# Linear attention and a gated MLP on one core: half units in pairs, twelve gated units, and TensorE for part of the first two batches

## The chip, the cores and the metric

The kernel runs on one core of one Trainium2 chip. The metric is the device time in microseconds of one execution. A core has five engines that the text names: TensorE (PE in the profile, with its weight loads as PEld), VectorE (DVE), ScalarE (ACT), GpSimd (POOL) and SyncE (SP, which issues nearly all DMAs here).

## What is computed

```python
q_s = softmax(q, axis=-1)            # over the 64 features of a row
k_s = softmax(k, axis=2)             # over the 576 rows of the sequence
kv  = einsum('bhsd,bhse->bhde', k_s, v)
x   = einsum('bhsd,bhde->bhse', q_s, kv)   # then (batch, row) x (8 heads * 64)
h   = x @ w_in
g   = h * sigmoid(beta * h)
out = g @ w_out
```

There are 8 batches, 8 heads, 576 rows and 64 features a head, so x has 4608 rows of 512; w_in is 512 x 2048 and w_out 2048 x 512. All inputs and the output are float32. The kernel writes g as (tanh(beta' h) + 1) h with the halves put into the constants.

## The kernel before, in words

**The work.** The sequence of a batch is split as row = 9 p + i, with p on 64 partitions and i from 0 to 8; two heads share the 128 partitions, so a batch has four blocks j of two heads. Of each batch, the rows i = 0 to 7 make one chunk of 512 tokens for the MLP, and the rows i = 8 of all batches together make one more (chunk 7, the tails; batch 7's own rows are chunk 8). A chunk has 16 units, one for each 128 columns of w_in: unit n multiplies xT by w_in into a PSUM bank (`st1`, line 758, operation `h_n`), ScalarE takes the tanh (`tanh`, line 774, `th_n`), VectorE forms the gated unit (`gate`, line 787, `g_n`) and TensorE multiplies it by w_out into the four output banks acc (`st2`, line 825, `o_n`). There are 9 x 16 = 144 units, each of four `h` matmuls and four `o` matmuls of 512 columns.

**The attention of batch b** goes through these operations: `ld_q`, `ld_k`, `ld_v` (line 259, each half a batch, 576 KB); `qmax` (360), `qsub` (376, GpSimd), `qexp` (383), `qsum` (406), `qrcp` (412, 413), `qnorm` (421, GpSimd) and then q transposed, `qT_b` (line 428): for batches 1 to 7 by one DMA that SyncE issues, for batch 0 by TensorE (`qtr`, line 442) with copies out of PSUM (`qtrev`); `qtrt_0` and `qtrtev_0` do its row i = 8. For k: `kmax` (462), `kred`, `ksmall`, `krep` (515, which lays the maximum, kmb, over the partitions), `ksub` (525), `kexp` (532). For batch 0 three of the four blocks' `ksub` are VectorE's and one GpSimd's, and `kswap_0` (479) is a small float32 product on TensorE. `vcast` makes v bfloat16. `kv_b` (556) gives k_s' v, `kvn_b` (575 to 578, VectorE) divides it, `x_b` (606) multiplies it with the transposed q, four `xev` copy the result to xT, and `xt_b` (645), `xtev` do the same for row i = 8.

**The order** is written out by hand in `ORDER`, a list of some 1200 names; each engine runs its own operations in that order and waits by semaphores. SyncE's order of loads, transposes and stores is part of it, as is the engine that a copy runs on (`=act`, `=dve`, `=pool`). Names with `fill` are matmuls on zeros or on exponentials that keep TensorE at work in the first 21 us; nothing reads them.

**Buffers.** PSUM has four banks `acc` for the outputs and a ring of four (`take`) for everything else: a `h` unit, a `kv` (two), an `x` half (two), an `xt` (two), a transposed q. A bank is free when the operation that empties it is done. `g` has NG = 8 buffers, so a gate waits for the `o` of the unit eight before; `th` has three. The output of a chunk is copied from acc to osb (`oev`) and stored (`st`, line 854) in two DMAs for each 128 tokens, one for each of the two rows i that the block holds.

**The first four units** (LEAD) work on halves of 256 tokens, since xT of batch 0 comes in halves: `h_n_half_x` are two of the four products, `th_n_half` and `g_n_half` take 256 columns each, and a unit holds one bank for both of its halves. The last eight units split their `o` by output block, and the last block (`oev_8_3`, `st_8_3`) by halves.

**The maximum of q in the first block** (SUMMED): for one of batch 0's parts ScalarE takes the maximum as a bias and sums as it goes (`q_exp_sum`, eight small activations for each block).

Of the kernel before, what the change touches and what calls it, by code (L numbers as in the profile page):

```python
# [22 lines left out]
krep_0_0, krep_0_1, ksub_0_2=dve, ksub_0_0=dve, qnorm_0_0_1=pool, vcast_0_j0=act, qexp_0_2_1, qsum_0_2_1,
vcast_0_j1=act, ksub_0_3=pool, vcast_0_j2=pool, fill_15, ld_q1_1, qrcp_0_1, fill_4, fill_14, qtrev_0_0_0=act,
kexp_0_2, qtr_0_0_1, kexp_0_3, kexp_0_0, ld_w0_1, ld_w0_0, ld_k1_1, ksub_0_1=dve, kexp_0_1, fill_16, kv_0_1, beta_ev,
kv_0_0, qmax_1_3, cast_w0_0_1=act, qmax_1_2, ld_w1_0, ld_w2_0, qnorm_0_1_0=pool, qnorm_0_1_1=pool, qtr_0_1_0,
qtr_0_1_1, fill_3, kvn_0, cast_w0_1_1=act, qtrev_0_1_0=act, qtrev_0_0_1=dve, x_0_0_1, x_0_0_0, xev_0_0_0=act,
cast_w0_1_0=pool, fill_5, qrcp_0_2, qtrev_0_1_1=dve, cast_w0_0_0=pool, xev_0_0_1=dve, qsub_1_1=pool, fill_7, x_0_1_1,
x_0_1_0, h_0_0_0, h_0_0_1, h_2_0_0, xev_0_1_0=act, qnorm_0_2_1=pool, kmax_1_3, xev_0_1_1=dve, th_0_0, g_0_0, h_3_0_0,
fill_6, cast_w2_0=pool, h_3_0_1, qexp_1_3, qnorm_0_2_0=pool, th_3_0, ld_w2_1, qexp_1_2, h_1_0_0, h_1_0_1, h_0_1_0,  # L30
h_2_0_1, cast_w1_0=pool, cast_w2_1=pool, ld_w1_1, h_2_1_0, h_2_1_1, h_0_1_1, h_3_1_0, th_1_0, h_1_1_0, ld_k1_0,
h_1_1_1, h_3_1_1, ld_w4_1, qsum_1_3, ld_w4_0, kmax_1_2, th_0_1, qsum_1_2, g_0_1, ld_w3_0, th_2_0, th_1_1, th_2_1,
ld_q1_0, ld_w3_1, o_0_0, th_3_1, g_3_0, g_2_0, g_2_1, qrcp_1_1, o_0_1, h_5, cast_w1_1=pool, qnorm_1_1=pool, ld_w6_1,
cast_w4_1=pool, g_3_1, g_1_0, g_1_1, kmax_1_1, kmax_1_0, kred_1, th_5, ksmall_1, h_4, g_5, o_1_0, th_4, h_6, th_6,
krep_1, g_4, o_1_1, h_7, o_2_0, o_2_1, o_3_0, cast_w4_0=pool, g_6, cast_w3_0=act, h_8, th_7, th_8, ld_w5_0, qmax_1_0,
qmax_1_1, ld_w6_0, ksub_1_0=pool, o_3_1, h_9, th_9, qsub_1_0=pool, h_11, o_4, cast_w3_1=act, o_5, o_6, g_7, o_7, g_8,
ld_w5_1, ld_q2_1, h_10, cast_w5_0=pool, cast_w6_1=act, th_11, ld_v1_1, qexp_1_1, ld_w7_0, o_8, g_11, qexp_1_0, g_9,
qsum_1_0, qsum_1_1, ksub_1_1=pool, cast_w6_0=act, th_10, qtrt_0, qtrtev_0_0=act, h_12, cast_w5_1=act, kexp_1_3, o_9,
h_14, kexp_1_0, th_12, qtrtev_0_1=dve, qrcp_1_0, kexp_1_1, th_14, g_10, qmax_2_2, qmax_2_3, qnorm_1_0=pool, h_15,
h_13, ld_v1_0, ld_w7_1, cast_w7_0=act, g_14, g_12, th_13, g_13, vcast_1_1=pool, qsub_2_1=pool, kexp_1_2, th_15, g_15,  # L40
vcast_1_0=pool, o_10, o_11, qexp_2_3, qexp_2_2, o_12, o_13, cast_w7_1=pool, qsum_2_3, kv_1_0, kv_1_1, o_14, qT_1,
kvn_1, qsum_2_2, x_1_1, x_1_0, xev_1_2=act, xev_1_0=dve, xev_1_3=dve, xev_1_1=act, qrcp_2_1, ld_q2_0, o_15, h_17_0,
qmax_2_0, ld_v2_1, ld_k2_1, ld_k2_0, h_17_1, qmax_2_1, oev_0_3=act, th_17, ld_q3_0, h_16_0, g_17, h_16_1, th_16,
g_16, ld_v2_0, ld_k3_0, h_18, th_18, oev_0_2=act, g_18, kmax_2_3, h_24, oev_0_0=act, h_21, th_21, kmax_2_0,
qnorm_2_1=pool, kmax_2_1, h_20, oev_0_1=act, qsub_2_0=pool, g_21, h_19, o_16, o_17, h_22, th_20, kmax_2_2, o_18,
qmax_3_0, g_20, th_19, g_19, ld_v3_0, qexp_2_1, th_24, th_22, kred_2, ksmall_2, vcast_2_1=pool, h_23, g_22, krep_2,
ld_k3_1, th_23, qmax_3_1, g_23, qexp_2_0, kmax_3_2, ld_q3_1, h_26, st_0_1, o_19, o_20, h_25, vcast_2_0=act, g_24,
qsum_2_1, kmax_3_3, ld_q4_0, o_21, h_27, qsum_2_0, th_26, o_22, vcast_3_0=pool, ksub_2_1=pool, kexp_2_2, th_25, g_26,
g_25, kexp_2_3, ksub_2_0=pool, th_27, o_23, g_27, ld_v3_1, o_24, o_25, xt_0, kexp_2_0, kexp_2_1, kv_2_0, kv_2_1,
xtev_0_0=act, xtev_0_1=act, h_30, h_28, kmax_3_0, qrcp_2_0, qnorm_2_0=pool, kmax_3_1, qsub_3_0=pool, qmax_3_2, kvn_2,  # L50
qmax_3_3, kred_3, th_30, th_28, g_28, st_0_3, qsub_3_1=pool, vcast_3_1=pool, h_29, o_26, ld_q4_1, h_31, st_0_0,
ld_k4_1, st_0_2, th_29, ksmall_3, g_29, g_30, qT_2, th_31, o_27, o_28, o_29, g_31, krep_3, x_2_1, xev_2_3=act, x_2_0,
xev_2_0=dve, xev_2_2=dve, qexp_3_1, ld_k4_0, o_30, o_31, xev_2_1=act, kmax_4_1, qexp_3_2, h_34, oev_1_2=act, th_34,
ksub_3_0=pool, ksub_3_1=pool, h_32, oev_1_1=dve, th_32, oev_1_3=act, qmax_4_1, h_33, oev_1_0=act, th_33, qexp_3_3,
g_34, g_32, ld_v4_1, h_35, qsum_3_1, ld_v4_0, th_35, st_1_1, ld_q5_1, h_37, h_36, qmax_4_3, kexp_3_3, g_33, th_36,
qmax_4_2, th_37, g_35, qmax_4_0, o_32, g_37, qsum_3_2, g_36, vcast_4_1=pool, vcast_4_0=pool, h_38, kexp_3_0, o_33,
th_38, h_39, qsum_3_3, qsub_4_1=pool, qexp_3_0, kexp_3_1, qsub_4_0=pool, th_39, g_39, qrcp_3_1, h_42, o_34, qsum_3_0,
# [58 lines left out]
def kernel(  # L116
# [629 lines left out]
    def st1(n, ks=(0, 1, 2, 3), h=None):  # L746
# [8 lines left out]
        if ("h", n) not in place:  # L755
            take(("h", n))
# [169 lines left out]
```

## Time and profile before

| | us |
|---|---|
| median of 3 runs | 293.31 (292.52 to 293.66) |
| the profiled execution's own time | 294.5 |
| its span, from the first to the last instruction | 292.7 |
| first `h` matmul on TensorE | 20.96 |
| last matmul ends | 288.04 |
| TensorE busy | 276.3 |
| VectorE, ScalarE, GpSimd busy | 199.6, 170.4, 130.7 |

Busy times are of the engine over the whole span. In a row of the order of time stand the start, the time, the engine, the line, the operation, what it writes and reads with the shape, the count, and in brackets the idle time of the engine just before it and what ended that. SPq, ACTq mean that the engine's sequencer issues a DMA. In a row of groups stand, after the bar, the busy time of all and the mean ns of one, then the idle time before them. PEclk is the granted share of TensorE's clock.

### The profile page before, as it was taken

Reading aid. Unit: us, or ns where it says so; the run is one execution under the profiler, and the core shown is the slowest. Engines: PE = TensorE matmul, PEld = TensorE weight load, DVE = VectorE, ACT = ScalarE, POOL = GpSimd, SP = SyncE. Lnnn points to the kernel's source line nnn. Section 1 sums busy time; section 2 is a strip of 40 time slices with the busy share of each in tenths; the row PEclk is TensorE's granted clock in tenths of the full one; section 3 lists DMA queues with packets and bytes.
Section 4 is the critical chain, followed back from the end, with each engine's and each line's share of the span. In section 5 each row is a group of like instructions: output and inputs, shape, how many; then the busy total and the mean of one; then the engine's idle time right before and its main releaser. Section 6 shows DMA issues by size and latency. Waiting matters only on the chain.

```text
span 292.7 us, 5174 instructions
## 1 busy us (share of the span) xinstructions
PE 276.3 (94%) x1922; PEld 128.7 (44%) x1951; DVE 199.6 (68%) x414; ACT 170.4 (58%) x297; POOL 130.7 (45%) x92
## 2 busy tenths in 40 slices
PE   7589999999999999996999999999999999999993
PEld 2255444444444544443344444444444444445551
DVE  3898867899799989774598968654754362456250
ACT  3687797866596656681375456845754255245342
POOL 5698986737987292661816473742002000000000
PEclk9889999999999999999799999999999999999999
DMA  7999999999954860699466908200410450005006
GB/s 247 392 391 385 386 380 208 394 383 357 231 185 155 209 215 0 176 229 304 164 204 226 179 23 164 61 2 0 111 34 2 81 125 21 0 1 129 17 0 143
DMA packets 39736, 50.60 MB, mean 173 GB/s; under 512 B 18576, under 2 KB 18848, under 8 KB 39712
## 3 DMA queue, kind: packets, MB, share of 16 engines
q1 hardware_dynamic: 39552, 50.15, 57.3%
q8 instruction: 15, 0.25, 0.3%
q10 hardware_dynamic: 160, 0.13, 0.2%
q14 instruction: 9, 0.07, 0.1%
HBM read 36.71 MB, written 9.44 MB: 158 GB/s over the span
## 4 chain that ended last, share of the span: by engine, by line
PE 73%; DMA 9%; DVE 6%; ACT 4%; issue 2%; SPq 2%; POOL 1%; POOLq 1%; ACTq 0%; DVEq 0%
PE hT L758 36%; PE acc L825 33%; DMA kf<-in_k_dram 6%; ACT th L774 2%; DMA qT<-qn 2%; DVE g L787 2%; DMA qf<-in_q_dram 1%; PE hT L606 1%; PE hT L556 1%; SPq L854 1%; ACT ek L532 1%; POOL kf L525 1%; DVE qs L406 1%; DMA out_dram<-osb 1%; POOLq L921 1%
## 5 line engine op out<-in xcount | busy, mean ns | idle before, releaser
L774 ACT ACTIVATE th<-hT,beta_c 128x512 bf16<-128x512 f32 (+1 forms) x148 | 97.1, 675 | 73.8 <-PE hT L758 59.4
L787 DVE SCALAR_TENSOR_TENSOR g<-th,hT 128x512 bf16<-128x512 bf16 (+1 forms) x148 | 94.8, 665 | 59.0 <-ACT th L774 56.7
L825 PE MATMUL acc<-w_out_b,g 128*128 128x512 bf16 x543 | 132.6, 381 | 1.3 <-issue 0.8
L758 PE MATMUL hT<-xT,w_in_b 128*128 128x512 bf16 (+1 forms) x519 | 119.1, 372 | 1.2 <-DVE g L787 0.7
L758 PEld LDWEIGHTS <-w_in_b 128*128 128x128 bf16 x592 | 57.6, 98 | 66.5 <-issue 1.2
L825 PEld LDWEIGHTS <-g 128*128 128x128 bf16 x560 | 53.8, 98 | 65.1 <-issue 4.3
L421 POOL TENSOR_TENSOR qn<-eq,qz 128x1152 bf16<-128x1152 bf16 (+2 forms) x20 | 34.6, 1738 | 50.8 <-DVE qz L413 35.0
L525 POOL TENSOR_TENSOR kf<-kf,kmb 128x1152 f32<-128x1152 f32 (+1 forms) x15 | 37.9, 2544 | 15.8 <-DVE kmb L515 10.0
L376 POOL TENSOR_TENSOR qf<-qf,qm 128x1152 f32<-128x1152 f32 (+2 forms) x19 | 33.3, 1768 | 20.1 <-DVE qm L360 13.2
L360 DVE TENSOR_REDUCE qm<-qf 128x9 f32<-128x576 f32 (+3 forms) x35 | 23.2, 688 | 8.3 <-DMA qf<-in_q_dram 8.2
L462 DVE TRANSPOSE_TENSOR_REDUCE km<-kf 128x18 f32<-128x576 f32 (+1 forms) x30 | 23.7, 803 | 1.8 <-DMA kf<-in_k_dram 1.6
L383 ACT ACTIVATE eq<-qf 128x576 bf16<-128x576 f32 (+2 forms) x33 | 20.9, 653 | 5.2 <-POOL qf L376 4.2
L406 DVE TENSOR_REDUCE qs<-eq 128x9 f32<-128x576 bf16 (+2 forms) x33 | 23.1, 706 | 0.1
L532 ACT ACTIVATE ek<-kf 128x576 bf16<-128x576 f32 x32 | 21.3, 684 | 2.4 <-POOL kf L525 2.3
L226 ACT CAST xT<-hT 128x512 bf16<-128x512 f32 x15 | 8.3, 587 | 18.7 <-PE hT L606 18.7
L228 POOL CAST va<-vf 128x1152 bf16<-128x1152 f32 (+1 forms) x14 | 14.9, 1080 | 7.7 <-DMA vf<-in_v_dram 7.7
L226 ACT COPY osb<-acc 128x512 f32<-128x512 f32 x23 | 13.0, 585 | 4.8 <-PE acc L825 2.2
L758 PE MATMUL hT<-xTt,w_in_b 128*128 128x512 bf16 x62 | 14.7, 379 | 0.1
L228 DVE COPY osb<-acc 128x512 f32<-128x512 f32 (+1 forms) x13 | 8.3, 659 | 7.0 <-PE acc L825 6.1
L349 PE MATMUL hT<-g,warm 128*128 128x512 bf16 x25 | 9.7, 512 | 1.6 <-POOL g L234 1.5
L228 DVE CAST xT<-hT 128x512 bf16<-128x512 f32 x13 | 8.3, 678 | 3.1 <-PE hT L606 3.0
L606 PE MATMUL hT<-qT,kvn 64*64 64x512 bf16 x56 | 5.4, 418 | 2.9 <-DVE kvn L578 2.5
(62 smaller groups left out, 106.5 us busy)
## 6 DMA issues: line engine op xcount, KB each, us to landing
qf<-in_q_dram SPq DMA_DIRECT2D x16, 576.0 KB, 5.0
kf<-in_k_dram SPq DMA_DIRECT2D x16, 576.0 KB, 7.3
vf<-in_v_dram SPq DMA_DIRECT2D x16, 576.0 KB, 7.6
out_dram<-osb SPq DMA_DIRECT2D x70, 128.0 KB, 2.4
wst<-in_moe_w_in_dram SPq DMA_DIRECT2D x8, 512.0 KB, 11.3
wst<-in_moe_w_out_dram SPq DMA_DIRECT2D x8, 512.0 KB, 11.1
out_dram<-osb SPq DMA_DIRECT2D x2, 64.0 KB, 2.0
out_dram<-osb ACTq DMA_DIRECT2D x2, 64.0 KB, 2.4
```

Of the source, the lines that this page charges most:

```text
L228: eng.tensor_copy(dst, src)
L360: dve.tensor_reduce(qm[:, j : j + n, i0:i1], qf[b % 2][:, j : j + n, i0:i1], axis=AX.X, op=ALU.max, negate=negate,)
L376: eng.tensor_tensor(x, x, m, ALU.subtract)
L406: dve.tensor_reduce(qs[:, i0:i1, j : j + n, 0:1], eq[:, i0:i1, j : j + n, :], axis=AX.X, op=ALU.add)
L421: eng.tensor_tensor(qn[b % 2][:, i0:i1, j : j + n, :], eq[:, i0:i1, j : j + n, :], z, ALU.mult)
L462: dve.tensor_reduce(km[:, j : j + n].rearrange("p j i e -> p (j i e)"), kf[b % 2][:, j : j + n].rearrange("p j i (e c) -> p (j i e) c", c=32),
L525: eng.tensor_tensor(x, x, m, ALU.subtract)
L532: act.activation(ek[b % 2][:, j : j + n], kf[b % 2][:, j : j + n], ACTF.Exp)
L758: pe.matmul(place[("h", n)][:, cols(h)], w_in_b[:, kt, u * P : (u + 1) * P], x[:, kt, cols(h)], start=(kt == 0), stop=(kt == KT - 1),)
L774: act.activation(th[n % 3][:, cols(h)], place[("h", n)][:, cols(h)], ACTF.Tanh, scale=beta_c[:, u : u + 1])
L787: dve.scalar_tensor_tensor(out=g[n % NG][:, cols(h)], in0=th[n % 3][:, cols(h)], scalar=1.0, in1=place[("h", n)][:, cols(h)], op0=ALU.add, ...
L825: pe.matmul(acc[t][:], g[n % NG][:, t * P : (t + 1) * P], w_out_b[:, u, :], start=(u == 0), stop=(u == NJ - 1),)
```

## The change

Seven things change, and the whole `ORDER` is written anew, so that nearly every operation has another place beside its neighbours.

1. *Half units in pairs.* For units 0 to 3, one bank holds the same half of two units (0 and 1, or 2 and 3). The two tanh's stay apart, since their scale differs; one gate of 512 columns serves both and waits for both.
2. *Twelve gated units* (NG from 8 to 12), kept as six tiles of two.
3. *Batch 1's q transposed by TensorE*: 16 transposes and two for row i = 8, with copies by VectorE and ScalarE; its DMA transpose goes.
4. *One store per block.* xT is written so that the two rows i of a pair alternate (`mixed`): tokens 2p and 2p + 1 of a block are neighbours in the output. A block of 128 tokens then goes out in one DMA in place of two.
5. *Part of k minus its maximum on TensorE*: for batch 0's blocks 0 and 1, `kin` puts k into PSUM by a float32 product with the identity, `kminus` adds the maximum times minus one, and `kexp` reads PSUM. The row i = 8 of both blocks takes a third bank (`kexp_0_n`). Block 2 is subtracted by GpSimd, block 3 by VectorE.
6. SUMMED is empty: the first block of q goes the way of the others.
7. In the new order more copies of v and of xT go to ScalarE; batch 6's q is asked for ahead of batch 4's transposed q, and batch 2's `kmax` stand ahead of `g_18`.

```diff
-    SUMMED = {(0, 1)}
+    SUMMED = set()
+    KPE = range(2)
-    NG = 8
+    NG = 12
...
-    g = [sbt(f"g{i}", [P, 512], BF16) for i in range(NG)]
+    gq = [sbt(f"g{i}", [P, 2, 512], BF16) for i in range(NG // 2)]
+    g = [gq[i // 2][:, i % 2] for i in range(NG)]
...
+    def k_in(j):
+        if j is None:
+            rhs = kf[0][:, 0 : len(KPE), NM, :]
+        else:
+            rhs = kf[0][:, j, 0:NM, :]
+        w = kn_bank() if j is None else acc[j][:]
...
+        pe.matmul(w, ident_f[:], rhs, start=True, stop=False)
+
+    def k_minus(j):
...
+            rhs = kmb[:, j].unsqueeze(1).to_broadcast((P, NM, D))
+        pe.matmul(kn_bank() if j is None else acc[j][:], minus[:], rhs, start=False, stop=True)
+
+    def k_exp_pe(j):
...
+        act.activation(ek[0][:, j, 0:NM], acc[j][:].rearrange("p (i d) -> p i d", d=D), ACTF.Exp)
...
+    def mixed(x):
+        return x.rearrange("p (t c i) -> p t i c", i=2, c=64)
...
-        cast(eng, xT[b % 2][:, j, :], place[("x", b, j)])
+        cast(eng, mixed(xT[b % 2][:, j, :]), place[("x", b, j)].rearrange("p (t i c) -> p t i c", i=2, c=64))
...
-        op(f"qT {b}", lambda b=b: q_tr_dma(b))
+        if b > 1:
+            op(f"qT {b}", lambda b=b: q_tr_dma(b))
+            continue
+        for J in range(2):
+            op(f"qtr {b} {J}", lambda b=b, J=J: q_tr(b, J, 0, NM))
+            op(f"qtrev {b} {J}", lambda e, b=b, J=J: q_tr_ev(b, J, 0, NM, e), "act")
...
+    def bank(n, h):
+        key = ("h", n) if h is None else ("hp", n // 2, h)
+        if key not in place:
+            take(key)
+        if h is None:
+            return place[key]
+        return place[key][:, 256 * (n % 2) : 256 * (n % 2) + 256]
...
+            out = gq[n // 2][:, :, cols(h)]
+            of = th[turn(n, h) % 3][:].rearrange("p (m t) -> p m t", m=2)
+            src = place[("hp", n // 2, h)].rearrange("p (m t) -> p m t", m=2)
+        dve.scalar_tensor_tensor(out=out, in0=of, scalar=1.0, in1=src, op0=ALU.add, op1=ALU.mult)
...
-        for s in range(2):
...
-            engs[s].dma_start(rows[:, f], osb[64 * s : 64 * s + 64, t, f])
+            rows = out[b * S : (b + 1) * S, :].rearrange("(p i) f -> p i f", i=NI)[:, 2 * t : 2 * t + 2]
+        eng.dma_start(rows[:, :, f], osb[:, t, f])
```

More of the change, by code (lines that the diff above doesn't have):

```diff
@@ L23 @@
[L23 to L27, printed above, removed]
@@ L33 @@
[L33 to L37, printed above, removed]
@@ L38 @@
[L38 to L57, printed above, removed]
```

308 lines of the change are left out of this document (197 added, 111 removed).

## The prediction

> **What bounds the kernel now.** I read the page first (busy shares and the clock), then the engines' busy time by stretch, then the chain of waits, and last the order of time on SyncE's queue around the one place where TensorE stands still.
>
> ```profile
> PE 276.3 (94%) x1922; PEld 128.7 (44%) x1951; DVE 199.6 (68%) x414; ACT 170.4 (58%) x297; POOL 130.7 (45%) x92
> ```
>
> TensorE is busy 94% of the span, so the end moves only by work added to it or by stretches in which it stands still or runs slowly. Cut at the first matmul of the MLP (20.96 us) and at the last matmul (288.04 us), the stretches show where those are (length, busy time of TensorE, its weight loads, VectorE, ScalarE and GpSimd, then TensorE's clock, the DMA share and GB/s):
>
> ```profile
> 0.00:20.96 20.96, 14.91 (x139) 6.77 (x140) 14.89 (x38) 12.94 (x35) 15.26 (x29) 0.92 0.95 341
> 20.96:54.00 33.04, 32.25 (x240) 16.05 (x240) 26.55 (x59) 25.87 (x43) 26.18 (x20) 1.00 1.02 346
> 54.00:81.00 27.00, 26.82 (x203) 12.17 (x205) 24.14 (x54) 17.72 (x31) 19.76 (x11) 1.00 1.00 336
> 81.00:136.30 55.30, 54.61 (x407) 25.33 (x411) 44.78 (x91) 36.95 (x63) 32.51 (x16) 1.00 0.65 172
> 136.30:142.70 6.40, 3.49 (x14) 1.03 (x14) 5.28 (x15) 1.64 (x3) 3.56 (x2) 0.73 0.93 353
> 288.04:292.70 4.66, 0.00 (x0) 0.00 (x0) 0.00 (x0) 0.37 (x1) 0.00 (x0) 1.00 0.62 151
> ```
>
> Outside the head (20.96 us of attention for batch 0, whose matmuls are mostly fills) and the tail (4.66 us), TensorE idles under 0.8 us in each long stretch. The exception is 136.3 to 142.7: 6.40 us, of which 2.91 idle, at a mean clock of 0.73. This is the one large sum to be had. SyncE's queue and the engines there:
>
> ```profile
> 122.61 7.40 SPq L428 DMA_TRANSPOSE qT<-qn  x1
> 130.05 2.52 SPq L854 DMA_DIRECT2D out_dram<-osb  x4
> 132.61 1.64 SPq L259 DMA_DIRECT2D qf<-in_q_dram  x3
> ...
> 136.74 1.41 DVE L360 TENSOR_REDUCE qm<-qf 128x9 f32<-128x576 f32 x2 [3.84 <-DMA qf<-in_q_dram]
> 138.88 0.40 PE L606 MATMUL hT<-qT,kvn 64*64 64x512 bf16 x1 [2.52 <-DVE kvn L578]
> 139.66 1.06 PE L606 MATMUL hT<-qT,kvn 64*64 64x512 bf16 x7 [0.39 <-DVE g L787]
> ```
>
> The transpose of batch 4's q holds SyncE for 7.40 us, four half stores for another 2.52, and only then is batch 6's q asked for. VectorE waits 3.84 us for it, because qmax_6_3 and qmax_6_2 stand before kvn_4 in its order; kvn_4 is late and TensorE waits 2.52 + 0.39 us. The clock follows:
>
> ```profile
> 12.92:16.33 3.41, 2.68 (x13) 1.48 (x13) 3.37 (x11) 2.85 (x6) 3.41 (x4) 0.50 1.03 384
> 135.80:139.21 3.41, 0.89 (x4) 0.17 (x3) 2.41 (x8) 0.00 (x0) 0.93 (x1) 1.00 1.04 391
> 139.21:142.63 3.42, 3.03 (x13) 0.92 (x12) 2.88 (x8) 1.64 (x3) 2.57 (x2) 0.50 0.86 324
> ```
>
> After 3.41 us with 0.89 us of work, the next 3.42 us run at 0.50, which loses 1.7. The stall costs 2.5 + 0.4 + 1.7 = **4.6 us**.
>
> **The change part by part.**
>
> *The stall.* In the new order the DMAs ahead of it differ. Both halves of batch 6's q are issued before the transpose of batch 4's q, the stores are half as many instructions, and on VectorE only qmax_6_2 stands near kvn_4, with its q loaded long before. After kv_4 TensorE now has o_48 to o_56 and ten h units before x_4 wants kvn_4 (before: o_59 and o_60, 8 matmuls or 1.7 us); twelve gated units allow that. I take the whole 4.6 us as gone (bounds -4.6 to 0). What is late next there: nothing within 5 us by the order.
>
> *The head.* The chain and the prices:
>
> ```profile
> 10.37 1.38 DVE L462 TRANSPOSE_TENSOR_REDUCE km<-kf 128x36 f32<-128x1152 f32 x1 [0.16 <-DMA kf<-in_k_dram]
> ...
> 13.38 0.67 ACT L226 CAST va<-vf 128x576 bf16<-128x576 f32 x1 [2.43 <-DMA vf<-in_v_dram]
> ...
> 13.85 0.20 DVE L515 STREAM_TRANSPOSE kmb<-kmx 128x64 f32<-128x64 f32 x1
> ...
> 15.21 2.61 ACT L532 ACTIVATE ek<-kf 128x576 bf16<-128x576 f32 x4
> ...
> 17.87 0.48 PE L556 MATMUL hT<-va,ek 64*64 64x65 bf16 x34 [0.36 <-ACT beta_c L332]
> 18.28 0.75 PE L442 MATMUL acc<-ident,qn 128*128 128x128 bf16 x8
> ...
> 27.15 1.02 PE L758 MATMUL hT<-xT,w_in_b 128*128 128x512 bf16 x4 [0.68 <-DVE g L787]
> ```
> ```profile
> L525 POOL TENSOR_TENSOR kf<-kf,kmb 128x576 f32<-128x576 f32 x1 | 1.4, 1404 | 0.0
> L226 ACT CAST w_out_b<-wst 128x1024 bf16<-128x1024 f32 x4 | 4.2, 1044 | 0.1
> L479 PE MATMUL hT<-kmr,swap 128*128 128x8 f32 x2 | 0.4, 252 | 1.6 <-DVE kmr L473 1.6
> L226 ACT CAST w_in_b<-wst 128x768 bf16<-128x768 f32 x2 | 1.6, 832 | 0.0
> L226 ACT CAST xT<-hT 128x512 bf16<-128x512 f32 x15 | 8.3, 587 | 18.7 <-PE hT L606 18.7
> ```
>
> The last half of batch 0's k is still the fourth 576 KB load, so the last kmax still starts near 10.4. Its small steps after that are less interleaved: kmb near 13.2, not 14.05. Then ScalarE is the limit. v's second half is there at 13.38; two casts of it at 0.67 take ScalarE to 14.7, four exponentials at 0.65 (2.61 / 4) and a small one to 17.5, where 17.82 stood before. Then kv runs most of both its halves (0.48 each) and ends near 18.4, as before; kvn likewise. ScalarE goes on with two casts of w (0.83 each), the small qexp, one qT copy and a small cast, about 3 us, and then xev_0_0_0 (0.59): the first h near 20.9. **Head -0.1 us** (bounds -0.8 to +0.9).
>
> k minus its maximum on TensorE (four fp32 products of 512 columns, two of 128) takes two of VectorE's three subtractions away; the third block goes to GpSimd (1.40, so 14.6).
>
> ```profile
> 28.76 0.86 PE hT L758 x4
> ```
>
> The trace has no wide fp32 product: bf16 ones of 512 columns are 0.22 us apart (0.86 / 4, from the chain), the fp32 one of 8 columns is two instructions of 0.25. Bounds 0.22 to 0.9 each; I take 0.6, as two passes are seen. kin runs before 11 us in place of fills; the two kminus, from 13.2, are ready at 13.8 and 14.4, and ScalarE, free at 14.7, does kexp_0_2 first: they cost nothing. If that cover is gone (0.9 each, and the clock at 0.50 as it stood at 12.92), the second comes at 16.8 and kv 0.6 us later. FP8 and Floating Point Precision, TensorE Precision Notes, in the Trainium skill says that true fp32 takes four passes; by it each would be an estimated 0.86 us at the full clock and ready at 14.9, still hidden. No run here shows it.
>
> *Half units in pairs.* Units 0 to 3 have four gates of 512 in place of eight of 256:
>
> ```profile
> L787 DVE SCALAR_TENSOR_TENSOR g<-th,hT 128x512 bf16<-128x512 bf16 x140 | 91.9, 680 | 58.1 <-ACT th L774 55.9 <-PE acc L825 1.2 <-PE hT L817 0.4
> L787 DVE SCALAR_TENSOR_TENSOR g<-th,hT 128x256 bf16<-128x256 bf16 x8 | 2.9, 408 | 0.9 <-ACT th L774 0.9
> L774 ACT ACTIVATE th<-hT,beta_c 128x256 bf16<-128x256 f32 x8 | 3.3, 471 | 0.0
> ```
>
> That is 8 x 0.41 - 4 x 0.68 = 0.5 us of VectorE saved, but a gate now waits for two tanh's. From 20.9 ScalarE has a cast (1.04), a small copy (0.15), an exponential (0.65) and three tanh's (0.47), so th_2_0 ends near 24.2 and g_2_0 near 24.9; h_5 starts there, and TensorE is through with the lead units (16 x 0.22 and a little) near 24.6. So the 0.68 us stall at 27.15 becomes one of about 0.3.
>
> *From 27 to 54 us.* Here the new order is tighter. cast_w3_0 stands on GpSimd behind qsub_1_1, which waits for qmax_1_2; o_4 wants it near 36.5 and TensorE is there 0.7 us sooner. qtrt_0's copies on VectorE, behind qtrev_1_0 and two qsum, hold a bank that h_13 wants (0.3). After x_1 four xev run on ScalarE alone, 4 x 0.59 = 2.3 us, beside 1.7 us of o_13, h_17_0 and h_16_0; two engines shared them before (0.6 lost, and some 0.4 ahead of kv_1). My sum of the stalls is 2.3, against 0.79 idle before, so +1.5; my dates lean to the late side as I added mean durations in a row where engines overlap, so I take **+1.1** (bounds 0 to +2.5). The eight transposes in 0.75 us, the last taking some 0.27, give 0.07 from one to the next: batch 1's 18 add **+1.2** to TensorE (0.9 to 2.0); the DMA transpose that goes was hidden, and batch 2's loads move up by its place on SyncE. After x_2 three xev and an exponential stand on ScalarE, beside o_30 and o_31: **+0.5** (0 to 0.9).
>
> xT is now written with every second element, and all 28 whole xev and the halves with it. No row has that form: between no cost and twice 0.59. The row with two separate runs (the halves into xT, 0.58) equals that with one, so I take nothing. SBUF — State Buffer, in its section on Door 1, in the Trainium skill has lines of 16 bytes, within which stepping bf16 is free up to 8 elements; by that it is nothing too. No run yet shows it.
>
> *Stores and tail.*
>
> ```profile
> 287.72 2.51 SPq L854 DMA_DIRECT2D out_dram<-osb  x4
> 288.07 0.37 ACT L226 COPY osb<-hT 128x256 f32<-128x256 f32 x1 [0.29 <-DMA out_dram<-osb]
> 288.47 0.48 ACTq L854 DMA_DIRECT2D out_dram<-osb  x1
> out_dram<-osb SPq DMA_DIRECT2D x2, 64.0 KB, 2.0
> out_dram<-osb ACTq DMA_DIRECT2D x2, 64.0 KB, 2.4
> ```
>
> At the end SyncE issues halves at 0.63 each until 290.23; the last, begun near 289.7, lands 2.0 later. With one store per block SyncE is clear by then, and the last store goes from ScalarE: 288.47 + 2.4 and a little more for 128 KB, near 291.0 in place of 291.7. **-0.7 us** (-0.9 to 0). Elsewhere stores are not waited for.
>
> **The sum**: -4.6 - 0.1 + 1.1 + 1.2 + 0.5 - 0.7 = -2.6 us on the span of 292.7, so 290.1. The profiled execution took 294.5; the median of the runs shown is 293.3, and the difference goes to that: **290.7 us**.
>
> **The rivals.**
>
> 1. *A jam in the first 81 us.* VectorE has 24.14 of 27.00 us between 54 and 81, and kvn_2 stands later in its order: 6.8 us more work ahead of it (mean durations). If the mean durations hold in a row, kvn_2 ends near 81.5 and TensorE comes near 81. All upper bounds there (2.5 + 2.0 + 0.9) are 2.6 us above my terms: 293.3. For it: VectorE and ScalarE are loaded highest here. Against: the same sum over all of before's VectorE work gives 217.7 us where 199.6 were busy.
>
> 2. *The stall only moves.* Another transpose holds loads or stores for which VectorE or ScalarE waits in order; nearest is qT_2, behind four loads and ahead of st_0_1 and st_0_0, for which oev_1_1 and oev_1_0 wait ahead of th_33 and th_34. At the price of the old stall: 290.7 + 4.6 = 295.3. Against: by the loads' bytes qT_2 is through near 75.5 and these stores land near 83, ScalarE wants them near 85.
>
> 3. *Slower: VectorE waits for batch 2's k.* All four kmax_2, kred_2, a qmax and ksmall_2 (about 5 us) now stand ahead of g_18, where kmax_2 followed g_18 before.
>
> ```profile
> 48.67 8.54 DMA kf<-in_k_dram
> ```
>
> Before, that k landed at 57.2. Now 16.1 MB stand up to it in the queue, which at 345 GB/s is 46.7 us, and kvn_1 ends near 49.5. From 50 us on, each microsecond later is one on TensorE, and past 2 us the slow clock adds 1.7. With landing at 55: 290.7 + 5 + 1.7 = 297.4. Against: only if SyncE is held by w5_1 or w7_0, whose buffers free at about 33 and 36.5.
>
> 4. *The change doesn't do what it says: strided evictions.* At twice 0.59, three batches (1, 2, 6) with little cover lose about 1.2 to 2.3 us each, some 4 in all: 294.7.
>
> **How the numbers follow.** Forecast 0.62, jam 0.17, moved stall 0.11, late k 0.05, stride 0.05. The low end is the sum of the good bounds with the whole stall gone: -4.6 - 0.8 + 0 + 0.9 + 0 - 0.9 = -5.4, 287.9. The high end reaches the moved stall, 295.3; beyond are late k, and half of the moved stall. A measurement of this kernel tells about 0.5% (1.5 us) from no change, so faster is under 291.8 and slower over 294.8. Of the forecast 0.06 lies in the same band, and of the jam 0.03 falls faster: faster 0.59, same 0.22, slower 0.19.
>
> **What would show it.** Right: no idle over 1 us on TensorE past 55 us and no clock under 1.00 after the head; first L758's successor near 20.9; SyncE's last store issued before 288.5; 18 more transposes near 50 ns to 70 ns apart. Wrong: a 0.50 clock window past 20 us, kmax_2 with a DMA ahead of it, xev above 0.65 us, fp32 products past 15 us, or over 3 us of idle on TensorE between 21 and 81.

## The result and the profile after

| | before | after |
|---|---|---|
| median, us | 293.38 (291.35 to 295.60, 20 runs) | 291.61 (290.35 to 293.67, 20 runs) |
| ratio after to before | | 0.9941 (0.9918 to 0.9964) |
| the profiled execution's own time, us | 294.5 | 292.57 |
| its span, us | 292.7 | 290.7 |
| first `h` matmul, us | 20.96 | 19.76 |
| last matmul ends, us | 288.04 | 286.96 |

The changed kernel is 1.8 us faster, and the interval excludes no change. Executions more than 1.5% above the fastest of their kernel are left out of the ratios, though they stand in the medians and ranges (of the last experiment's kernel only three of twelve are within that).

On the page of the kernel after, TensorE is busy 97% of the span, where 94% stood before:

```profile
PE 281.5 (97%) x1981; PEld 131.4 (45%) x1981; DVE 196.9 (68%) x402; ACT 179.2 (62%) x300; POOL 125.9 (43%) x88
```

The busy time by stretch of the kernel after, cut as in the prediction (length, busy time of TensorE, its weight loads, VectorE, ScalarE and GpSimd, then TensorE's clock, the DMA share and GB/s):

```profile
19.76:26.00 6.24, 4.76 (x26) 3.27 (x26) 3.14 (x8) 3.29 (x7) 4.43 (x6) 0.73 1.02 356
26.00:54.00 28.00, 27.98 (x228) 13.54 (x227) 23.69 (x54) 23.72 (x38) 15.74 (x9) 1.00 1.04 382
54.00:81.00 27.00, 27.00 (x202) 12.30 (x199) 25.55 (x55) 21.36 (x36) 20.85 (x10) 1.00 0.81 231
81.00:136.30 55.30, 54.03 (x413) 24.38 (x416) 47.05 (x100) 41.09 (x68) 40.04 (x21) 1.00 0.80 237
136.30:142.70 6.40, 6.40 (x36) 2.76 (x29) 3.40 (x6) 5.48 (x9) 4.17 (x3) 1.00 0.60 161
286.96:290.70 3.74, 0.00 (x1) 0.00 (x0) 0.00 (x0) 0.37 (x1) 0.00 (x0) 1.00 0.56 200
```

The stretch from 136.30 to 142.70, where TensorE idled 2.91 us and ran at 0.73, is now full at the full clock. Two others are not. From 19.76 to 26.00 TensorE idles 1.48 us and its mean clock is 0.73, and between 81 and 136.30 it idles 1.27. The holes in them are new, and the experiments are about them.

**The hole at the start.** The order of time of the kernel after, TensorE and the four copies of batch 0's x into xT:

```profile
18.44 1.00 PE L667 MATMUL acc<-qT,kvn 64*64 64x256 bf16 x16
18.97 0.74 ACT L230 CAST xT<-acc 128x512 bf16<-128x512 f32 x1
19.08 0.72 DVE L232 CAST xT<-acc 128x512 bf16<-128x512 f32 x1
19.76 0.27 PE L861 MATMUL hT<-xT,w_in_b 128*128 128x256 bf16 x1 [0.33 <-ACT xT L230]
19.97 0.71 DVE L232 CAST xT<-acc 128x512 bf16<-128x512 f32 x1
20.73 0.81 PE L861 MATMUL hT<-xT,w_in_b 128*128 128x256 bf16 x6 [0.70 <-DVE xT L232]
21.54 0.73 DVE L232 CAST xT<-acc 128x512 bf16<-128x512 f32 x1 [0.87 <-ACT eq L397]
22.32 2.08 PE L861 MATMUL hT<-xT,w_in_b 128*128 128x256 bf16 x10 [0.78 <-DVE xT L232]
```

By the order the lone matmul at 19.76 is the first product of `h_2_0_0`, on xT's block 0, first half. Its second product reads block 2, first half, which ScalarE's copy at 18.97 (`xev_0_0_0`, blocks 0 and 2 together) had written by 19.71. Yet it starts at 20.73, when VectorE's copy of blocks 1 and 3 (`xev_0_1_0`, 19.97) ends. Of the six matmuls the last is the first product of `h_3_0_0`; its second again reads block 2, first half, and again waits, for the copy at 21.54 (`xev_0_1_1`, blocks 1 and 3, second half). That copy's input was there at 19.44, but it starts only when the six matmuls end. These are waits for data that nothing here reads. The row's own word for the last one, ScalarE's eq, is only the latest event by the profile.

What followed in this execution was half the clock (windows of the kernel after):

```profile
19.16:22.57 3.41, 1.61 (x18) 1.00 (x13) 2.51 (x7) 2.21 (x4) 3.41 (x5) 1.00 1.02 338
22.57:25.98 3.41, 3.41 (x19) 2.35 (x17) 1.21 (x3) 1.68 (x4) 1.62 (x2) 0.50 1.03 381
```

After 3.41 us with 1.61 of work, the next 3.41 run at 0.50, which loses 1.7. It isn't so in every execution: 13 of the 20 had a mean clock of 0.997 or more and took 290.35 to 291.95 us (median 290.87), the 7 at 0.994 or less 291.94 to 293.67 (median 292.4). The Trainium skill, TensorE: Matmul & The Clock Gate, Part 1, has a window of 3413 ns that runs freely and doesn't start with the kernel, so a fixed hole can fall into one window or over two. The two groups are as that would make them; that the phase decides is not shown by a run here.

**The hole at 87 us.** The order of time of the kernel after, SyncE's queue and what comes of it:

```profile
73.99 4.14 SPq L442 DMA_TRANSPOSE qT<-qn  x1
...
78.25 1.03 SPq L273 DMA_DIRECT2D kf<-in_k_dram  x2
...
79.33 0.59 SPq L954 DMA_DIRECT2D out_dram<-osb  x1
...
86.26 0.58 ACT L230 COPY osb<-acc 128x512 f32<-128x512 f32 x1 [2.30 <-DMA out_dram<-osb]
...
87.47 0.69 DVE L896 SCALAR_TENSOR_TENSOR g<-th,hT 128x512 bf16<-128x512 bf16 x1 [2.05 <-ACT th L879]
88.21 2.09 PE L861 MATMUL hT<-xT,w_in_b 128*128 128x512 bf16 x8 [1.23 <-DVE g L896]
```

The transpose of batch 2's q holds SyncE for 4.14 us, two loads of k follow, then `st_0_1`. ScalarE waits 2.30 us for that store, since `oev_1_1` writes the same part of osb; the tanh's stand behind it, then a gate, and TensorE idles 1.23.

**The tail.** The last stores on SyncE in the kernel after:

```profile
284.90 2.60 SPq L954 DMA_DIRECT2D out_dram<-osb  x4
```

SyncE issues four stores in 2.60 us, where eight took 4.96; it is clear at 287.50, 0.54 after the last matmul. The tail is 3.7 us, where 4.7 stood.

**The account** of the profiled executions: the first `h` -1.20; the stall at 136 -4.6; idle time from the first `h` to 54 us 1.50 in place of 0.79, +0.7; the slow clock in the lead +1.7; the transposes +1.0 (measured below); the hole at 87 +1.2; the tail -1.0. That makes -2.2, and the spans differ by 2.0.

### The profile page after: what moved, and what is told of

It is laid out like the page before. It is cut to its first block, busy times and chain, and to the rows that moved or that the text cites. A ratio compares the mean times of both kernels' runs of the same rounds, so it can differ in the third digit from the quotient of the medians.

```text
span 290.7 us, 5187 instructions
## 1 busy us (share of the span) xinstructions
PE 281.5 (97%) x1981; PEld 131.4 (45%) x1981; DVE 196.9 (68%) x402; ACT 179.2 (62%) x300; POOL 125.9 (43%) x88
## 4 chain that ended last, share of the span: by engine, by line
PE 83%; DMA 7%; POOL 3%; DVE 2%; ACT 1%; SPq 1%; issue 1%; POOLq 0%; ACTq 0%
PE hT L861 40%; PE acc L927 38%; DMA vf<-in_v_dram 2%; DMA out_dram<-osb 2%; DMA qf<-in_q_dram 2%; PE hT L617 1%; POOL qn L435 1%; PE hT L667 1%; SPq L273 1%; PE hT L919 1%; PE acc L919 1%; POOL qf L390 1%; DVE qm L374 1%; DVE km L478 0%; ACT th L879 0%
## 5 line engine op out<-in xcount | busy, mean ns | idle before, releaser
L896 DVE SCALAR_TENSOR_TENSOR g<-th,hT 128x512 bf16<-128x512 bf16 x144 | 94.7, 680 | 69.2 <-ACT th L879 64.8
L861 PE MATMUL hT<-xT,w_in_b 128*128 128x512 bf16 (+1 forms) x528 | 120.8, 377 | 3.1 <-DVE xT L232 1.5
L374 DVE TENSOR_REDUCE qm<-qf 128x9 f32<-128x576 f32 (+2 forms) x34 | 23.2, 705 | 4.9 <-DMA qf<-in_q_dram 4.9
L230 ACT CAST xT<-hT 128x512 bf16<-128x512 f32 x22 | 14.7, 740 | 12.3 <-PE hT L667 11.3
L230 ACT COPY osb<-acc 128x512 f32<-128x512 f32 (+1 forms) x25 | 13.9, 587 | 10.4 <-PE acc L919 4.0
L232 POOL CAST va<-vf 128x1152 bf16<-128x1152 f32 (+1 forms) x11 | 12.0, 1106 | 14.2 <-DMA vf<-in_v_dram 14.1
L363 PE MATMUL hT<-g,warm 128*128 128x512 bf16 x26 | 8.1, 470 | 1.5 <-POOL g L238 1.5
L232 DVE COPY osb<-acc 128x512 f32<-128x512 f32 x11 | 7.3, 686 | 2.6 <-PE acc L927 2.5
L232 DVE CAST xT<-hT 128x512 bf16<-128x512 f32 x6 | 4.3, 720 | 4.7 <-PE hT L667 4.6
L617 PEld LDWEIGHTS <-ek 64*64 64x64 bf16 x576 | 5.8, 106 | 2.2 <-issue 1.3
```

Of the source, the lines that this page charges most:

```text
L230: act.copy(dst, src)
L232: eng.tensor_copy(dst, src)
L374: dve.tensor_reduce(qm[:, j : j + n, i0:i1], qf[b % 2][:, j : j + n, i0:i1], axis=AX.X, op=ALU.max, negate=negate,)
L861: pe.matmul(w, w_in_b[:, kt, u * P : (u + 1) * P], x[:, kt, cols(h)], start=(kt == 0), stop=(kt == KT - 1),)
L896: dve.scalar_tensor_tensor(out=out, in0=of, scalar=1.0, in1=src, op0=ALU.add, op1=ALU.mult)
```

## The experiments

The theory: the change is worth what the stall at 136 was, and most of the rest is given back by two waits that the new code and order bring, a false one in the lead and a queued store at 87 us. The rival: the gain comes from the sum of the parts (twelve gated units, TensorE's share of the head, one store per block), and the holes are only where TensorE waits for whatever is late.

| kernel | median, us | ratio to before |
|---|---|---|
| before, batch 6's q asked for early | 290.05 | 0.9875 (0.9841 to 0.9909) |
| before, 12 gated units | 294.77 | 1.0026 (1.0002 to 1.0051) |
| after, half copies split | 289.81 | 0.9879 (0.9841 to 0.9917) |
| after, own column order of x, two stores | 293.00 | 0.9991 (0.9960 to 1.0023) |
| after, two stores early | 291.28 | 0.9902 (0.9866 to 0.9939) |
| **after, both repairs** (split, stores early) | **288.80** | **0.9848 (0.9793 to 0.9903)** |
| repaired, transposes twice | 289.55 | 0.9842 (0.9801 to 0.9884) |
| repaired, batch 1's q by DMA | 297.63 | 1.0122 (1.0080 to 1.0164) |
| the same DMA, later | 295.60 | 1.0040 (1.0015 to 1.0064) |
| repaired, no subtraction on TensorE | 291.12 | 0.9892 (0.9849 to 0.9935) |
| repaired, batch 6's q behind the transpose | 300.98 | 1.0204 (1.0150 to 1.0258) |
| after, stores early, own column order | 295.72 | 0.9941 (0.9889 to 0.9993) |

### The stall alone

The kernel before, with two names of its order moved:

```diff
+ld_q6_1, ld_q6_0,
 ld_v5_1, ld_v5_0, qT_4,
...
-ld_q6_1,
...
-ld_q6_0,
```

> The kernel before with one thing moved: both loads of batch 6's q are issued ahead of batch 5's v and of the transpose of batch 4's q, the rest as it was. Theory (the prediction's): the stall at 136.3 us is VectorE waiting for that load ahead of kvn_4, worth 2.5 + 0.4 us of idle and 1.7 us of slow clock; it goes, the span falls by 4.0 to 4.6 us to about 288.4, ratio to the kernel before 0.985, and no clock of 0.50 near 139 us. Rival: something else is late there at once (the exponentials of batch 5, the loads of v pushed behind q), so under 1.5 us is won and TensorE idles at another place between 134 and 150 us.

Measured: 290.05 us. Windows of this kernel:

```profile
81.00:136.30 55.30, 55.30 (x415) 25.41 (x412) 47.73 (x99) 37.19 (x64) 34.07 (x17) 1.00 0.65 182
136.30:142.70 6.40, 6.40 (x36) 2.71 (x35) 4.40 (x11) 3.21 (x6) 4.96 (x4) 1.00 0.78 235
```

The stall and its slow clock are gone, and the kernel is some 3.7 us faster (1.25% of 293.8), near the 4.6 of the trace; the two profiled spans differ by 4.6 (288.1 for 292.7). So this one move gives twice what the whole change gives, and the other parts together cost 1.6 us by the medians (1.9 by the ratios). The rival falls.

### The false wait in the lead

First, the changed kernel with each half copy of x made two, one for each block:

```diff
-        x = xT[b % 2][:].rearrange("p (J c) (t n i) -> p c J t i n", c=2, i=2, n=64)
-        w = place[("x", b, jp, h)].rearrange("p (J t i n) -> p J t i n", J=2, t=2, i=2)
-        cast(eng, x[:, jp, :, 2 * h : 2 * h + 2], w)
+        w = place[("x", b, jp, h)]
+        for J in range(2):
+            x = mixed(xT[b % 2][:, 2 * J + jp, 256 * h : 256 * h + 256])
+            cast(eng, x, w[:, 256 * J : 256 * J + 256].rearrange("p (t i c) -> p t i c", i=2, c=64))
```

> The changed kernel with each copy of half an x into xT (four of 512 columns in batch 0) made two of 256, one for each block of rows of xT, so that what a copy writes doesn't span the other half of the block between. Theory: the 0.70 and 0.78 us for which TensorE idles at 20.0 and 21.5 us are waits for copies whose data it doesn't need, and the slow clock from 22.6 us follows from them; both go: 1.5 us less, 3.2 in executions that had the slow clock, a median near 289.4; the copies cost VectorE 0.3 us more in all. Rival: the wait moves to the next step (tanh and gates of the first units), less than 0.6 us is won, and the slow clock stays.

Measured: 289.81 us. TensorE in the lead, in order of time:

```profile
19.23 6.05 PE L862 MATMUL hT<-xT,w_in_b 128*128 128x256 bf16 x41
```

In this execution there is no hole of over 0.1 us left and no slow clock (one of the six took 292.13 us), though the copies still write in steps and are twice as many. Second, the changed kernel with xT in its own column order, by one copy per half as before, and with two stores per block:

```diff
-        cast(eng, mixed(xT[b % 2][:, j, :]), place[("x", b, j)].rearrange("p (t i c) -> p t i c", i=2, c=64))
+        cast(eng, xT[b % 2][:, j, :], place[("x", b, j)])
...
+        cast(
+            eng,
+            xT[b % 2][:].rearrange("p (J c) t -> p c J t", c=2)[:, jp, :, 256 * h : 256 * h + 256],
+            place[("x", b, jp, h)].rearrange("p (J t) -> p J t", J=2),
+        )
...
+        for s in range(2):
```

> The changed kernel with change 4 undone: x is written to xT in rows without steps, as in the kernel before, and each block is stored by two DMAs. Same order. Theory: the stepped copies cost 0.15 us each on ScalarE (0.74 against 0.59) but lie beside matmuls, so nothing is won but in the first copies of batch 0 (0.15), and the tail is 0.7 to 0.9 us longer; with twice as many stores ahead of loads on SyncE the wait at 87 us grows by up to 1: 0.5 to 1.5 us more than the changed kernel. Rival: the stepped copies are on the path of x_1, x_2 and x_6, and undoing them wins 1 us or more.

Measured: 293.00 us, so 1.4 above the kernel after. That is in the expected range, but by other terms, as the two views show. TensorE's lead in order of time, and then the window behind the last matmul:

```profile
19.83 5.47 PE L863 MATMUL hT<-xT,w_in_b 128*128 128x256 bf16 x39 [0.17 <-ACT xT L230]
```
```profile
284.40:290.50 6.10, 0.00 (x1) 0.00 (x0) 0.00 (x0) 0.37 (x1) 0.00 (x0) 0.68 0.58 142
```

The wait is gone here as well, with joint copies. So it takes both: one instruction for two blocks, and the stepped write. The last matmul comes 2.6 us sooner than in the kernel after (284.40 for 286.96), and eight half stores then take the tail to 6.1. In these two executions change 4 costs 2.6 up to the last matmul, where 0.15 was expected, and gives 2.4 behind it, where 0.7 to 0.9 was expected. Of the 2.6, 1.7 is the slow clock of this execution of the kernel after; without it change 4 would gain an estimated 1.5, near the 1.4 of the medians. Why the joint stepped copy is ordered against the blocks between its two was not tried; the likely reason, argued only, is that with its additional dimensions the area that it writes is taken as all from its first to its last column.

### The store at 87 us

```diff
-kvn_2, st_0_3, qsub_3_1=pool, qT_2,
+kvn_2, st_0_3, qsub_3_1=pool, st_0_1, st_0_0, qT_2,
```

> The changed kernel with two stores of chunk 0 (blocks 1 and 0) issued ahead of the transpose of batch 2's q in place of behind it. Theory: the 1.23 us for which TensorE idles at 87 us come from ScalarE's 2.30 us wait for the first of these stores, ahead of th_33; it goes, with the 0.2 us after it: 1.2 to 1.5 us less than the changed kernel, about 290.2 in the median. Rival: oev_1_1 isn't the limit there, the next wait (a gate, ScalarE's four copies) takes over and less than 0.5 us is won.

Measured: 291.28 us. The window of this kernel, and the same one of the kernel after:

```profile
84.00:90.00 6.00, 6.00 (x29) 2.66 (x28) 5.69 (x13) 5.54 (x11) 3.82 (x2) 1.00 0.87 327
```
```profile
84.00:90.00 6.00, 4.73 (x22) 2.02 (x21) 3.52 (x8) 3.74 (x8) 2.31 (x2) 1.00 0.95 368
```

The 1.27 us are gone; the span is 289.3 for 290.7, as expected. The median moved by 0.3 only, in place of the expected 1.2 to 1.5, over twelve executions from 289.43 to 296.00; the ratios (0.9902 for 0.9941) are 1.1 us apart, though their intervals overlap. So the wait's cause is shown in the trace, and its price is not settled by the times.

### Both repairs

> The changed kernel with both repairs at once: the half copies of x as two casts each, and the two stores of block 0 issued ahead of the transposing DMA of batch 2. Theory (two separate waits, one in the lead at 20 to 22 us, one at 87 us): the gains add; the span is that of the split alone (288.0) less the idle time that its trace still shows at 83.4 us (1.13), so about 286.9, and the time about 288.6. Rival (the time is set by what TensorE may do per stretch, and a hole that is closed only opens another): within 0.4 of the split alone, 289.4 to 290.2.

Measured: 288.80 us, span 286.9, both as the first theory had them. Windows:

```profile
19.63:26.00 6.37, 6.24 (x44) 4.25 (x44) 5.86 (x15) 5.98 (x14) 4.72 (x6) 1.00 1.00 339
...
81.00:136.30 55.30, 55.30 (x418) 25.14 (x417) 46.05 (x99) 42.49 (x71) 41.01 (x21) 1.00 0.74 222
```

TensorE has no stall left between the first `h` and the end, where 0.15 us of idle time remain. This version beats both kernels. Against the kernel before with its stall repaired it is 1.25 us shorter by the medians and 0.8 by the ratios, whose intervals overlap, and two of its six executions took 292.38 and 293.02 us; that difference is not shown.

### Twelve gated units

```diff
-    NG = 8
+    NG = 12
```

> The kernel before with 12 gated units in place of 8 and nothing else. Theory (no gate waits for a unit to come free on the path, and the wait at 136 us is for loads): within 0.5 us of the kernel before, ratio 0.998 to 1.002. Rival (the units of slack let TensorE run on over the wait at 136 us): 2 us or more below it, ratio under 0.993.

Measured: 294.77 us, no gain. The order of time of this kernel shows the stall in its place:

```profile
135.66 1.41 DVE L360 TENSOR_REDUCE qm<-qf 128x9 f32<-128x576 f32 x2 [3.56 <-DMA qf<-in_q_dram]
137.79 0.40 PE L606 MATMUL hT<-qT,kvn 64*64 64x512 bf16 x1 [2.23 <-DVE kvn L578]
```

Twelve units in the old order buy nothing. The new order needs them: `g_11` stands in it before the last `o` of unit 3, whose buffer it would take with eight.

### The transposes, doubled

```diff
-        for i in range(n):
+        for i in [x for x in range(n) for _ in range(2 if b == 1 else 1)]:
```

> The kernel with both repairs, and each of batch 1's 20 TensorE transposes issued twice into the same place. Theory (they lie in a stretch where TensorE has no idle time, so each costs its 64 ns): 1.1 to 1.5 us above the kernel with both repairs, about 290.1. Rival (TensorE would wait there anyway for the copies or for a bank, so the transposes fill idle time): within 0.4 of it.

The expectation counts 20 by the row of the repaired kernel, but two of them are row i = 8 of batch 0: 18 were doubled. The transposes in the order of time, repaired kernel, then doubled:

```profile
33.50 0.61 PE L458 MATMUL hT<-ident,qn 128*128 128x128 bf16 x8
...
43.26 0.73 PE L458 MATMUL hT<-ident,qn 128*128 128x128 bf16 x10
```
```profile
33.01 1.06 PE L458 MATMUL hT<-ident,qn 128*128 128x128 bf16 x16
...
43.08 1.28 PE L458 MATMUL hT<-ident,qn 128*128 128x128 bf16 x20
```

The first group takes 0.45 us more, the second 0.55: 1.00 for 18, or 56 ns each. The median rose by 0.75 us (289.55), which the ratios don't show (0.9842 for 0.9848). The two profiled spans are alike (287.0 and 286.9), but the doubled kernel's first `h` came 0.3 sooner (19.33), which is scatter of the head, so I go by the local times: the transposes of batch 1 cost TensorE about 1.0 us, in a stretch where it has no idle time (0.02 us from 26 to 54 us in the repaired kernel).

### Batch 1's q by DMA again

```diff
-qtr_1_1, qtrt_1,
+qT_1,
...
-        if b > 1:
+        if b > 0:
             op(f"qT {b}", lambda b=b: q_tr_dma(b))
```

> The kernel with both repairs, and batch 1's q transposed by one DMA again, issued where TensorE's second set of transposes stood. Theory of the prediction (the 20 transposes cost TensorE what they last, 1.28 us, and the DMA would have been hidden): 1.0 to 1.3 us below the kernel with both repairs, about 287.4. Rival (the transposing DMA holds SyncE until the loads ahead of it have landed, 3 to 7 us, so batch 1's v and batch 2's k and q come later and TensorE waits for the copies of batch 1's x or for kv): 0 to 4 us above it, with idle TensorE between 45 and 60 us.

Measured: 297.63 us, 8.8 above the repaired kernel (8.1 by the ratios), and beyond the rival's range. The order of time:

```profile
42.62 2.80 SPq L441 DMA_TRANSPOSE qT<-qn  x1
...
45.47 0.57 SPq L272 DMA_DIRECT2D vf<-in_v_dram  x1
...
50.18 1.15 POOL L231 CAST va<-vf 128x1152 bf16<-128x1152 f32 x1 [6.50 <-DMA vf<-in_v_dram]
51.38 0.71 PE L616 MATMUL hT<-va,ek 64*64 64x65 bf16 x36 [6.20 <-POOL va L231]
```

SyncE stands before the transpose until GpSimd has scaled q, at 42.6, and the second half of v is asked for at 45.47; in the repaired kernel its load was issued at 32.56. TensorE waits 6.20 us for it, runs at half the clock from then to 54.65, and 2.1 us more go at 85 us, where the next transpose is late in turn. Placed behind v, k and half of q of the next batches:

> The kernel with both repairs, batch 1's q by one transposing DMA again, this time issued as late as x of batch 1 allows, behind batch 1's v, batch 2's k and the first half of its q. Theory (the 8.8 us that the DMA cost at its early place came from v alone, queued behind it on SyncE): TensorE saves 1.28, nothing waits, and the time is 0.9 to 1.3 us below the kernel with both repairs. Rival (SyncE is held until GpSimd has scaled q, at about 42.6 us, and then for the DMA itself, so the last weights and batch 3's loads come 5 us or more later wherever it is put): 1 to 5 us above it.

Measured: 295.60 us, 6.8 above (5.6 by the ratios), again beyond the rival's range.

```profile
42.90 5.54 SPq L441 DMA_TRANSPOSE qT<-qn  x1
...
52.01 1.07 PE L666 MATMUL hT<-qT,kvn 64*64 64x512 bf16 x8 [4.37 <-DMA qT<-qn]
```

Now TensorE waits for the transposed q itself, 4.37 us, and runs at half the clock from 50.50 to 57.35. At neither place was the DMA hidden: in this order x of batch 1 comes too early for it. A saving of 1.0 us stands against 6.8 and 8.8 of loss.

### No subtraction on TensorE

```diff
-    KPE = range(2)
+    KPE = range(0)
...
-ksub_0_3=dve, ... ksub_0_2=pool,
+ksub_0_3=pool, ksub_0_2=dve, ksub_0_1=dve, ksub_0_0=dve,
```

> The kernel with both repairs, and no part of k minus its maximum on TensorE: VectorE subtracts for three pairs, GpSimd for the fourth, as in the kernel before. Theory (the subtraction on TensorE takes work off VectorE, which the first h waits for): the first h comes 0.6 to 1.2 us later than in the kernel with both repairs, and the time is 0.6 to 1.2 above it. Rival (the earlier start comes from the order of the loads and from ScalarE's shorter list): within 0.4 of it.

Measured: 291.12 us, 2.3 above the repaired kernel (1.3 by the ratios), where 0.6 to 1.2 was expected. The order of time of this kernel in the head:

```profile
12.45 2.08 DVE L542 TENSOR_TENSOR kf<-kf,acc 128x576 f32<-128x576 f32 x3
...
15.07 4.06 POOL L434 TENSOR_TENSOR qn<-eq,qz 128x512 bf16<-128x512 bf16 x4 [0.45 <-DVE qz L426]
16.17 0.40 PE L457 MATMUL acc<-ident,qn 128*128 128x128 bf16 x4 [2.63 <-POOL qn L434]
...
21.49 1.23 PE L861 MATMUL hT<-xT,w_in_b 128*128 128x256 bf16 x8
```

The exponentials of k are done at 16.2, as with TensorE's help. What is late is q: three subtractions, 2.08 us, stand ahead of the sums of q's exponentials on VectorE, so GpSimd scales q at 15.07 (13.99 in the kernel after), TensorE waits 2.63 us for it and runs at half the clock from 16.93 to 20.34, and the first `h` comes at 21.49, for 19.63 in the repaired kernel. That is 1.9 of the loss, and TensorE also waits 0.8 us at 80 us for batch 2's transposed q. The names were put back by hand and the order isn't tuned for them, so I take the 2.3 as an upper bound of what TensorE's share is worth.

### The stall put back

```diff
-ld_q6_1, ... ld_q6_0, ... qmax_6_2, ... qT_4,
+qT_4, ld_q6_1, ld_q6_0, ... qmax_6_2, qmax_6_0,
```

> The kernel with both repairs, with the two loads of batch 6's q put back behind the transposing DMA of batch 4, and VectorE's first maximum over that q behind them. Theory (the place of these two loads made the stall at 136 us of the kernel before): SyncE is held about 5 us there, VectorE waits for q, and the time is 3 to 6 us above the kernel with both repairs. Rival (the 12 gated units give enough slack to cover such a wait): less than 1 us above it.

Measured: 300.98 us, 12.2 above (10.5 by the ratios), about twice the upper end of what was expected. The order of time and a window of this kernel:

```profile
116.53 5.13 SPq L442 DMA_TRANSPOSE qT<-qn  x1
...
121.71 10.00 SPq L273 DMA_DIRECT2D qf<-in_q_dram  x3
126.01 0.75 DVE L374 TENSOR_REDUCE qm<-qf 128x9 f32<-128x576 f32 x1 [8.18 <-DMA qf<-in_q_dram]
...
128.83 1.87 PE L862 MATMUL hT<-xT,w_in_b 128*128 128x512 bf16 x4 [7.86 <-DVE g L897]
```
```profile
123.87:134.11 10.24, 5.28 (x13) 1.87 (x13) 7.23 (x11) 1.84 (x3) 0.00 (x0) 0.50 0.43 141
```

SyncE is held 5.13 us, but VectorE comes to the maximum of q at 117.8, before SyncE is free at all, and waits 8.18. Gates stand behind it, and twelve units cover 3 us of that. TensorE idles 7.86 us, and the three windows from 123.87 on are at 0.50, with 5.28 us of work in them, which loses another 2.6. Of all that was undone here, the place of these two loads cost the most, though it isn't the two loads alone: the edit moves `qmax_6_2` as well.

### The store early, in the own column order

The two edits of before together: x in its own order with two stores per block, and `st_0_1`, `st_0_0` ahead of `qT_2`.

> The changed kernel with the two stores of block 0 issued early, and without the mixed column order: x copied in its own order by one copy per half, two stores per tile of the output. Theory (the false wait in the lead comes with the stepped write of the joint copies, and one store per tile shortens the end only): TensorE's last matmul ends within 0.4 us of the kernel with both repairs (282.5), the end behind it takes 5.5 to 6.1 us in place of 4.4, and the time is 1.2 to 2.3 above it. Rival (the joint copies make the wait whatever the order of the columns): idle time of 1 us or more at 20 to 22 us, as in the changed kernel.

Measured: 290.32 to 296.56, mostly near 295.7. The lead is as in the first of the two (idle 0.1 of 6.47 us, from the window), so the rival falls once more:

```profile
19.53:26.00 6.47, 6.37 (x44) 4.22 (x44) 5.74 (x12) 5.71 (x13) 4.55 (x6) 1.00 1.02 352
```

The shortest, 290.32, is within the expected range of 290.0 to 291.1; ten of the twelve took 294.63 or more. The profiled execution took 296.56: its last matmul ends at 288.33, not near 282.5, and the end behind it takes 6.5 us. It has waits for a transpose at 77.6 and for stores at 156 us, which the shortest can't have had in that size; what sets them apart stays open, and so does the price of two stores per block there.

## Why the prediction was right

The time, 291.6, lies within the range and 0.9 above the forecast. By its steps:

- **The stall, -4.6.** Right, in size and cause: the clock window and both waits are gone, and the two loads moved alone take 3.7 us from the kernel before. The prediction put it to the loads' place, and twelve units as what allows it; the first is shown, the second only so far as the order can't do without them.
- **The head, -0.1.** Too small: -1.20, beyond the bound of -0.8. It is clear of the scatter: the first `h` comes at 20.48 to 21.51 us in the three profiles of the old order, at 19.23 to 19.96 in the ten of the new order with TensorE's share. The step that failed is "ScalarE is the limit", with four exponentials ending at 17.5. In the trace the last big one ends at 16.3: v was cast from 12.10, where I took 13.38 of the profile before, and kmb was ready at 12.54, not 13.2, since VectorE could start on the last half of k 0.6 sooner (9.78). And the limit without TensorE's share is VectorE, by way of q's scale.
- **fp32 products, 0.6 each and hidden.** Hidden, but longer:

```profile
13.07 1.88 PE L572 MATMUL acc<-kmb,minus 128*128 128x512 f32 x4
...
15.22 0.39 PE L572 MATMUL hT<-kmb,minus 128*128 128x128 f32 x2
```

Four recorded instructions are two products, 0.94 us each, at the full clock; that is above my bound of 0.9. The estimate of 0.86 by the four passes that the Trainium skill has (FP8 and Floating Point Precision, TensorE Precision Notes) was nearer than mine.

- **27 to 54 us, +1.1.** Wrong: TensorE idles 0.02 us there. Sums of mean durations in a row put the copies late; the prediction named that lean and still took 1.1 of its 1.5.
- **The lead, where "the 0.68 us stall at 27.15 becomes one of about 0.3".** The wait for a gate did go, to nothing, but ahead of it TensorE idled 1.48 us and, in this execution, lost 1.7 to the slow clock. The step that failed is that "xT is now written with every second element ... I take nothing". As a price it holds on the path, though the rows are not as I took them, nor as the Trainium skill, SBUF — State Buffer, Door 1, would have it (lines of 16 bytes, stepping bf16 free up to 8 elements):

```profile
L230 ACT CAST xT<-hT 128x512 bf16<-128x512 f32 x22 | 14.7, 740 | 12.3 <-PE hT L667 11.3 <-PE hT L709 0.8
...
L232 DVE CAST xT<-hT 128x512 bf16<-128x512 f32 x6 | 4.3, 720 | 4.7 <-PE hT L667 4.6
```

ScalarE's copy went from 587 to 740 ns, VectorE's from 678 to 720; in the kernel with x in its own order they are 591 and 677. The trace speaks against the page there, unless the cost comes from the dimensions that the stepped copy has more, which no run here tells apart. The real cost is the false wait, which no sum of durations could show.

- **Transposes, +1.2.** Mis-sized a little: 1.0.
- **x_2's evictions, +0.5.** None: TensorE idles 0.00 from 54 to 81 us. The first rival, a jam before 81, didn't come (the sum of VectorE's work that stood against it is 213.7 by the rows of groups, not 217.7).
- **The second rival** came by its mechanism and at its place: `qT_2` ahead of `st_0_1`, waited for by `oev_1_1` ahead of the tanh's. The store landed at 86.2, not 83. Its price was 1.2 us, not 4.6: ScalarE waited 2.30, the clock stayed, and slack took the rest.
- **The third rival**, late k of batch 2, didn't come; nor did the fourth, strided evictions on the path.
- **The tail, -0.7.** -0.96 in the profiled executions. It scatters: in five of the nine profiled kernels with one store per block it is 4.3 to 4.6 us, in the other four 3.6 to 3.8, with the same issues.

Of the signs that the prediction set for itself, SyncE is clear in time (287.50) and the transposes are 56 ns apart. But three of its signs of being wrong came as well: half the clock from 22.57 to 25.98, copies into xT above 0.65 us, and an fp32 product past 15 us; and TensorE idled over 1 us past 55 us, at 87.

So the largest term, the stall, was right by its mechanism, and the rest is near by luck, as a sum of errors: a head 1.1 better and nothing lost from 27 to 81 (1.6 better), against a lead that was 2.4 and a store that was 1.2 worse. The slow clock's 1.7 of that is in the profiled execution; by their mean clocks, 13 of the 20 seem to be without it.

## What to carry to other kernels

When an order is rewritten, price each wait by itself: here two names in SyncE's list, moved alone, were worth twice the whole change, and a transpose in a queue is priced by what stands behind it, not by its own time. Look for matmuls that wait for a copy whose data they don't read, and split or reshape the copy. Count the slow clock that may follow a stall: here 1.8 us idle in 3.41 were followed by half the clock, the 1.23 us at 87 were not. Time several executions, because it may come or not.

## What was not expected of the hardware

- A stepped bfloat16 write of 512 columns costs ScalarE 740 ns in place of 587 to 591, and VectorE 720 in place of 677.
- The transposing DMA of one batch's q, the same in shape and size, held SyncE from 2.7 us (after's at 139.4) to 8.7 (at 124.6 in the kernel before with early q).
- 1.61 us of work in a window of 3.41 (the kernel after, in its lead) was followed by half the clock, as 0.89 was before.
- An fp32 product of 512 columns took 0.94 us, as two recorded instructions, one of 128 columns 0.39.
- With the same instructions up to there, the first `h` came at 19.23 to 19.63 us in six kernels.
